# A decode kernel of attention and an MLP on one core: 16 of 128 partitions of two weight loads move from SyncE's DMA queue to GpSimd's

## The chip, the cores and the metric

The kernel runs on one core of a Trainium2 chip. The metric is the device time of one execution in microseconds (us). Three runs of the kernel before gave 213.38, 213.41 and 213.50 us; their median is 213.41 us.

## The reference, cut to what matters

There are four rows (a batch of 4, one token each) of width D = 576. After a layer norm, the result is the sum of the row, an attention part and an MLP part:

```python
xn = _layernorm(x)
return x + _A_ref(xn, A_k_cache, A_v_cache, A_wq, A_wo) + _B_ref(xn, B_w1, B_w2, B_w3, B_w4)

# attention: 32 query heads, 16 kv heads of width 128, a window of the last 2048 keys
p = softmax((xn @ wq) @ k.T * Dh ** -0.5);  o = p @ v;  return o @ wo
# MLP: the sequence has length 1, so that the shifted part hs is zero
x1 = x + hs
return x1 + _gelu(_layernorm(x1) @ w3) @ w4        # w3: 576 x 4608, w4: 4608 x 576
```

Nothing is shared between rows but the weights, and every byte of keys, values and weights is used once. All tensors are bf16.

## The kernel before, in words

**What is loaded.** All loads but that of x are issued by SyncE (SP in the profile), in one queue, in the order in which the program needs them. Large tiles (`wq`, `k`, `w3a`, `w3b`, `v`, `w4_end`) come from one pool, `big`, with four buffers of 4 MiB (NBUF = 4), so that a load is issued when the buffer that it takes has been given up by its last reader. The order of the pool is wq, k0, w3a, k1, w3b, k2 to k7, then eight pairs of value heads, then `w4_end`. `w3b` takes the buffer of `wq`, and k5 takes the buffer of `w3b`.

**The stages.** First q = xn @ wq (line 236). Then eight key tiles (line 512 on): each is transposed on VectorE in four pieces (line 297) and multiplied with q on TensorE (line 304). The MLP is put between the first key tiles. With tile 0, `w3a` is multiplied (first two of the four rows per partition, and the tail of w3; line 465 by way of `g_piece`); with tile 1, `w3b` (the second two rows), and then come gelu (line 467) and the first 12 of 36 rows per partition of w4, by `mlp_out` (line 395), which adds to an accumulator in PSUM. After the keys come softmax (line 309), the 16 value heads (line 384), `wo` in four pieces, and the other 24 rows of w4 in five pieces, of which the last four arrive at the very end (line 504 by way of `quad_out`). The sum is cast (line 579) and stored (line 580).

**The lines that the change touches.** For n == 1, line 521 takes a buffer for `w3b`, line 522 loads w3's second two rows per partition (`load_rows`, line 136: 128 partitions of 18,432 bytes, 2304 KB), and line 523 loads the first 12 rows of w4 behind them in the same buffer (`load_w4`, line 482: 128 partitions of 13,824 bytes, 1728 KB). Their readers are `g_piece` (line 526, over w3) and `mlp_out` (line 529, over w4[0]). GpSimd (POOL) issues no DMA before the change; it has eight short instructions, the last at 8.3 us.

**What sets the order.** In the part around the change the tile framework places the waits. A transfer waits for the last reader of the buffer it overwrites, and a matmul waits for the transfers that write what it reads. Within an engine, instructions run in program order. From line 539 on, TensorE's order is written out by hand.

Of the kernel before, what the change touches and what calls it, by code (L numbers as in the profile page):

```python
# [20 lines left out]
def kernel(  # L21
# [19 lines left out]
    nc = tc.nc  # L41
    P = 128
    B, Sq, D = A_x.shape
# [4 lines left out]
    F = B_w3.shape[1]  # L48
# [56 lines left out]
    def k_load(bp, kq, last=False):  # L105

        t = big.tile([P, CK, Dh], BF16, tag="big", name=f"k{bp}{kq}")
        lo = Sk - W + kq * 4 * CK
        src = k_rows[MT * bp:MT * bp + MT, lo:lo + 4 * CK, :].rearrange("m (q c) d -> m q (c d)", q=4)
        cuts = 2 if last else 1  # L110
        for a in range(cuts):
            n = CK * Dh // cuts
            nc.sync.dma_start(out=t[:].rearrange("p c d -> p (c d)")[:, a * n:(a + 1) * n], in_=src[:, :, a * n:(a + 1) * n])
        return t
# [12 lines left out]
    w3_src = B_w3[0:KJ * P, :].rearrange("(p j) f -> p j f", j=KJ)  # L127
    w4_src = B_w4.rearrange("(e m i) n -> e m i n", e=2, i=NFH)
# [3 lines left out]
    JR = 2  # L132

    def load_rows(t, a, src, j, n):

        nc.sync.dma_start(out=t[:, a:a + JR * n].rearrange("p (j n) -> p j n", j=JR), in_=src[:, j:j + JR, :])
        return [t[:, a + i * n:a + (i + 1) * n] for i in range(JR)]

    def load_tail(t, a, w, n):
        nc.sync.dma_start(out=t[:, a:a + n // 2], in_=w[KJ * P:D, :].rearrange("r (e f) -> (r e) f", e=2))  # L140
        return t[:, a:a + n // 2]
# [142 lines left out]
    def k_scores(n):  # L284

        bp, kq = K_order[n]
        kn = K_tiles.pop(n)
        if n == 0:
            S.extend(ps_s.tile([P, 512], F32, tag="S", name=f"S{g}") for g in range(4))
        C2 = CK // 2  # L290

        kt = [ktp.tile([P, C2, G, 2, 2], BF16, tag="kt", name=f"kt{n}{e}") for e in range(2)]
        last = n == len(K_order) - 1
        for i in range(4):
            a, e = divmod(i, 2) if last else (i % 2, i // 2)
            c0 = a * C2 // 2
            nc.vector.transpose(out=ap32(kt[e], c0 * 2 * G, [[2 * G, C2 // 2], [1, 2], [2, G]]),  # L297
                                in_=ap32(kn, c0 * 4 * G + e * G, [[4 * G, C2 // 2], [2 * G, 2], [1, G]]))
        for e in range(2):
            for t in range(2):  # L300
                y = 2 * e + t
                for m in range(NM):
                    c = 32 * (m % 4)
                    nc.tensor.matmul(out=S[kq][c:c + 32, :].rearrange("p (c q l) -> p c q l", q=4, l=2),  # L304
                                     lhsT=qz[:, bp, m, y, :], rhs=kt[e][:, :, 4 * m:4 * m + 4, :, t],
                                     start=(bp == 0 and m < 4 and y == 0), stop=(bp == 1 and m >= 4 and y == NY - 1),
                                     skip_group_check=True)
# [150 lines left out]
    def g_piece(t, j):  # L458
        for fc in range(NF):
            e, i = divmod(fc, NFH)  # L460
            if j < KJ:
                lhsT, rhs = t[:, e * (F // 2) + i:(e + 1) * (F // 2):NFH], ln2T[:, j, :]
            else:
                lhsT, rhs = t[:, i:F // 2:NFH], ln2T[:, KJ + e, :]
            nc.tensor.matmul(out=gp[:, fc, :], lhsT=lhsT, rhs=rhs, start=False, stop=False, skip_group_check=True)  # L465

    def gelu():
        xs = const.tile([P, NF, B], F32, name="g_x")
        nc.vector.tensor_copy(out=xs[:], in_=gp)
        u = const.tile([P, NF, B], F32, name="g_u")  # L470
        nc.vector.tensor_tensor(out=u[:], in0=xs[:], in1=xs[:], op=ALU.mult)
        nc.vector.tensor_scalar(out=u[:], in0=u[:], scalar1=GA, scalar2=1.0, op0=ALU.mult, op1=ALU.add)
        nc.vector.tensor_tensor(out=u[:], in0=u[:], in1=xs[:], op=ALU.mult)
        nc.scalar.activation(out=u[:], in_=u[:], func=ACT.Tanh, scale=GC)
        nc.vector.tensor_scalar(out=u[:], in0=u[:], scalar1=0.5, scalar2=0.5, op0=ALU.mult, op1=ALU.add)
        nc.vector.tensor_tensor(out=gT[:], in0=u[:], in1=xs[:], op=ALU.mult)
        nc.vector.tensor_copy(out=gTq[:, :, 0:G:NB], in_=gT[:, NFH:NFH + NQR, :])

    def load_w4(t, j0, e, i0, cuts):
        parts = []  # L480
        for m in cuts:
            nc.sync.dma_start(out=t[:, j0:j0 + m, :], in_=w4_src[e, :, i0:i0 + m, :])
            parts.append((t[:, j0:j0 + m, :], e, i0, m))
            j0 += m
            i0 += m
        return parts
# [20 lines left out]
    def mlp_out(t, e, i0, n, one=False):  # L507
        for i in range(n):
            acc_matmuls(gT[:, e * NFH + i0 + i, :], lambda a, z, i=i: t[:, i, a:z], 0 if one else i % 2)


    for n in range(len(K_order)):
        if n > 0:
            K_tiles[n] = k_load(*K_order[n], last=(n == len(K_order) - 1))
        w3 = []
        if n == 0:
            w3_a = big.tile([P, BIG], BF16, tag="big", name="w3a")
            w3 = list(enumerate(load_rows(w3_a, 0, w3_src, 0, F)))
            w3.append((KJ, load_tail(w3_a, JR * F, B_w3, F)))
        elif n == 1:  # L520
            w3_b = big.tile([P, BIG], BF16, tag="big", name="w3b")
            w3 = list(enumerate(load_rows(w3_b, 0, w3_src, JR, F), JR))
            w4 = load_w4(w3_b[:, JR * F:JR * F + 12 * D].rearrange("p (i n) -> p i n", n=D), 0, 0, 0, (12,))
        k_scores(n)
        for j, t in w3:
            g_piece(t, j)
        if n == 1:
            gelu()
            mlp_out(*w4[0], one=True)
# [81 lines left out]
```

## Time and profile before

| what | value |
|---|---|
| median of three runs | 213.41 us |
| span of the profiled execution, first to last instruction | 212.0 us |
| bytes moved, mean rate over the span | 87.32 MB, 412 GB/s |
| share of 16 DMA engines' span taken by SP's queue (q1) | 96.8% |
| busiest compute engine | DVE, 128.2 us (60%) |
| POOL | 1.8 us, 8 instructions |

The profiled execution has no time of its own beside its span; 213.41 - 212.0 = 1.4 us is what lies around the span (the launch ahead of the first instruction, and the end). A page of the profile gives each engine's busy time, a row of digits over 40 equal slices of the span, the DMA queues, the chain of work that ended last, and groups of instructions by line. "DMA share" is the mean busy share of the core's 16 DMA engines. The trace also holds a record of every DMA packet: its queue, size, start and duration, but not the engine that it ran on.

### The profile page before, as it was taken

The page shows a single profiled execution, that of the slowest core. Times are in us where ns is not written, and L with a number is a line of the kernel's source. Part 1 is how long each engine was busy: PE and PEld are TensorE (multiplying, and loading weights), DVE is VectorE, ACT ScalarE, POOL GpSimd, SP SyncE. Part 2 cuts the span into 40 slices and gives each one's busy share as a digit, 9 for nine tenths or more (in the row PEclk, how much of TensorE's full clock was granted, in tenths as well). Part 3 has the DMA queues.
Part 4 walks back from the last instruction along what each step waited for, and adds up shares of the span by engine and source line. Part 5 has one row for each costly group of instructions (what it writes and reads, how often), then busy time and mean ns, then how long its engine had stood idle before and what let it go on. Part 6 is the DMA issues. An engine that isn't in the chain of part 4 may idle for free. (4 is left out here: it accounts for less than half of the span.)

```text
span 212.0 us, 2539 instructions
## 1 busy us (share of the span) xinstructions
PE 98.4 (46%) x1071; PEld 50.5 (24%) x1071; DVE 128.2 (60%) x225; ACT 17.4 (8%) x35; POOL 1.8 (1%) x8
## 2 busy tenths in 40 slices
PE   1442059429903333423333421968573644555573
PEld 0111027408301011101111101734231321212241
DVE  7812592095349898979699916968475322145240
ACT  0004100000000000000000058730000000000000
POOL 2100000000000000000000000000000000000000
PEclk9999999999999999999999999999787555555555
DMA  7999999999999999999999999999999999999980
GB/s 261 427 457 433 411 442 454 392 420 460 420 420 457 411 445 433 408 451 399 433 427 420 436 415 432 436 423 423 426 430 417 434 415 438 423 427 419 423 356 18
DMA packets 5943, 87.32 MB, mean 412 GB/s; under 512 B 681, under 2 KB 685, under 8 KB 1453
## 3 DMA queue, kind: packets, MB, share of 16 engines
q1 hardware_dynamic: 5924, 87.17, 96.8%
q8 instruction: 8, 0.13, 0.3%
q14 instruction: 3, 0.02, 0.0%
q10 hardware_dynamic: 8, 0.00, 0.0%
HBM read 87.17 MB, written 0.00 MB: 411 GB/s over the span
## 5 line engine op out<-in xcount | busy, mean ns | idle before, releaser
L297 DVE STREAM_TRANSPOSE kt<-k 128x2048 int32<-128x2048 int32 x32 | 71.0, 2278 | 17.5 <-DMA k<-in_A_k_cache_dram 17.5
L304 PE MATMUL S<-kt,qz 128*32 128x512 bf16 x256 | 30.4, 622 | 56.9 <-DVE kt L297 56.9
L384 PE MATMUL O<-v,PZ 128*32 128x512 bf16 x256 | 23.6, 506 | 15.1 <-DMA v<-in_A_v_cache_dram 15.1
L304 PEld LDWEIGHTS <-qz 128*32 128x32 bf16 x256 | 9.5, 127 | 74.0 <-issue 67.5
L413 DVE TENSOR_SCALAR osum<-O,diag 128x128 f32<-128x128 f32 x16 | 5.6, 348 | 28.8 <-PE O L384 28.8
L415 DVE SCALAR_TENSOR_TENSOR osum<-O,diag,osum 128x128 f32<-128x128 f32 x48 | 16.5, 345 | 0.9
L384 PEld LDWEIGHTS <-PZ 128*32 128x32 bf16 x256 | 7.5, 116 | 22.5 <-DMA v<-in_A_v_cache_dram 12.6
L346 PE MATMUL pt<-ident,prs 128*128 128x128 bf16 x64 | 6.5, 287 | 10.1 <-DVE prs L342 10.1
L321 ACT ACTIVATE E<-S,nb 128x256 f32<-128x256 f32 x8 | 4.5, 704 | 69.9 <-DVE nb L318 69.9
L425 PEld LDWEIGHTS OT<-sel,osum 128*128 128x128 f32 x32 | 6.6, 258 | 13.5 <-issue 7.1
L425 PE MATMUL OT<-sel,osum 128*128 128x8 f32 x32 | 8.1, 326 | 3.4 <-DVE osum L415 3.4
L395 PE MATMUL ACC<-wo,onx 128*4 128x288 bf16 x64 | 4.5, 434 | 8.7 <-DVE onx L444 8.7
L346 PEld LDWEIGHTS <-prs 128*128 128x128 bf16 x64 | 5.8, 131 | 11.5 <-ACT prs L340 9.4
L342 DVE TENSOR_SCALAR prs<-E,rdm 128x512 bf16<-128x512 f32 x12 | 7.8, 801 | 0.0
L465 PEld LDWEIGHTS <-w3a 128*128 128x128 bf16 x108 | 6.9, 161 | 1.7 <-issue 1.7
L465 PE MATMUL ACC<-ln2T,w3a 128*128 128x4 bf16 x108 | 7.0, 202 | 0.0
L316 DVE TENSOR_REDUCE mx<-S 128x1 f32<-128x512 f32 x4 | 2.7, 681 | 5.4 <-PE S L304 5.4
L236 PE MATMUL qp<-wq,xnT 128*8 128x512 bf16 x32 | 3.8, 621 | 4.5 <-DMA wq<-in_A_wq_dram 4.5
L567 ACT COPY sums<-ACC 64x288 f32<-64x288 f32 x1 | 0.4, 393 | 64.5 <-PE ACC L395 64.5
L251 DVE CAST q_rows<-qp 128x256 bf16<-128x256 f32 x4 | 1.5, 420 | 5.9 <-PE qp L236 3.9
L340 ACT ACTIVATE prs<-E,rdm 128x512 bf16<-128x512 f32 x4 | 4.9, 1404 | 0.8 <-DVE rdm L328 0.8
L465 PEld LDWEIGHTS <-w3b 128*128 128x128 bf16 x72 | 4.5, 160 | 0.8 <-issue 0.8
(91 smaller groups left out, 68.1 us busy)
## 6 DMA issues: line engine op xcount, KB each, us to landing
v<-in_A_v_cache_dram SPq DMA_DIRECT2D x16, 2048.0 KB, 26.4
k<-in_A_k_cache_dram SPq DMA_DIRECT2D x7, 4096.0 KB, 30.6
wo<-in_A_wo_dram SPq DMA_DIRECT2D x4, 1152.0 KB, 29.8
wq<-in_A_wq_dram SPq DMA_DIRECT2D x2, 2048.0 KB, 12.9
k<-in_A_k_cache_dram SPq DMA_DIRECT2D x2, 2048.0 KB, 25.0
w3a<-in_B_w_dram SPq DMA_DIRECT2D x1, 2304.0 KB, 27.0
w3b<-in_B_w_dram SPq DMA_DIRECT2D x1, 2304.0 KB
w3b<-in_B_w_dram SPq DMA_DIRECT2D x1, 1728.0 KB, 34.6
```

The source lines that it names most:

```text
L297: nc.vector.transpose(out=ap32(kt[e], c0 * 2 * G, [[2 * G, C2 // 2], [1, 2], [2, G]]), in_=ap32(kn, c0 * 4 * G + e * G, [[4 * G, C2 // 2], ...
L304: nc.tensor.matmul(out=S[kq][c:c + 32, :].rearrange("p (c q l) -> p c q l", q=4, l=2), lhsT=qz[:, bp, m, y, :], rhs=kt[e][:, :, 4 * m:4 * ...
L321: nc.scalar.activation(out=E[:, :, g, x:GK:2].rearrange("p (c l) q -> p c q l", l=2), in_=S[g][:, 256 * x:256 * (x + 1)].rearrange("p (c q ...
L340: nc.scalar.mul(out=dst, in_=src, mul=rdm[:, b:b + 1])
L342: nc.vector.tensor_scalar_mul(out=dst, in0=src, scalar1=rdm[:, b:b + 1])
L346: nc.tensor.transpose(out=tp[:, cc, :], in_=pr[:, half * HC + cc, :, :, :].rearrange("p g k b -> p (g k b)"), identity=ident[:])
L384: nc.tensor.matmul(out=bank[G * j:G * j + G, :], lhsT=PZ[:, hp, c0:c0 + NI, :].rearrange("p c m -> p (c m)"), rhs=vn[:, c0:c0 + NI, :].rea ...
L395: nc.tensor.matmul(out=ACCS[half][o0:o0 + B, 0:DH], lhsT=lhsT, rhs=rhs_cols(q * DH, (q + 1) * DH), start=False, stop=False, skip_group_che ...
L413: nc.vector.tensor_scalar_mul(out=osum[:], in0=bank[:, 0:Dh], scalar1=diag[:, 0:1])
L415: nc.vector.scalar_tensor_tensor(out=osum[:], in0=bank[:, i * Dh:(i + 1) * Dh], scalar=diag[:, i:i + 1], in1=osum[:], op0=ALU.mult, op1=AL ...
L425: nc.tensor.matmul(out=OT[:, NB * o:NB * o + NB], lhsT=osum[:], rhs=sel[:], start=True, stop=True, skip_group_check=True)
L465: nc.tensor.matmul(out=gp[:, fc, :], lhsT=lhsT, rhs=rhs, start=False, stop=False, skip_group_check=True)
```

## The change

```diff
@@ -519,8 +519,16 @@
             w3.append((KJ, load_tail(w3_a, JR * F, B_w3, F)))
         elif n == 1:
             w3_b = big.tile([P, BIG], BF16, tag="big", name="w3b")
-            w3 = list(enumerate(load_rows(w3_b, 0, w3_src, JR, F), JR))
-            w4 = load_w4(w3_b[:, JR * F:JR * F + 12 * D].rearrange("p (i n) -> p i n", n=D), 0, 0, 0, (12,))
+            PM = P - 16
+            n2, n4 = JR * F, 12 * D
+            nc.sync.dma_start(out=w3_b[0:PM, 0:n2].rearrange("p (j n) -> p j n", j=JR), in_=w3_src[0:PM, JR:2 * JR, :])
+            nc.sync.dma_start(out=w3_b[0:PM, n2:n2 + n4].rearrange("p (i n) -> p i n", n=D), in_=w4_src[0, 0:PM, 0:12, :])
+            for p in range(PM, P):
+                nc.gpsimd.dma_start(out=w3_b[p:p + 1, 0:n2].rearrange("p (j n) -> p j n", j=JR), in_=w3_src[p:p + 1, JR:2 * JR, :])
+            for p in range(PM, P, 4):
+                nc.gpsimd.dma_start(out=w3_b[p:p + 4, n2:n2 + n4].rearrange("p (i n) -> p i n", n=D), in_=w4_src[0, p:p + 4, 0:12, :])
+            w3 = [(JR + i, w3_b[:, i * F:(i + 1) * F]) for i in range(JR)]
+            w4 = [(w3_b[:, n2:n2 + n4].rearrange("p (i n) -> p i n", n=D), 0, 0, 12)]
         k_scores(n)
         for j, t in w3:
             g_piece(t, j)
```

SyncE's two loads keep partitions 0 to 111. Partitions 112 to 127 come in GpSimd's queue: sixteen transfers of one partition (18,432 bytes each, w3), then four of four partitions (4 x 13,824 bytes each, w4). What is read, and where it is put, is the same.

## The prediction

> **What bounds the kernel now.** I read the page's slices first: is any engine busy all along?
>
> ```profile
> DVE  7812592095349898979699916968475322145240
> PEclk9999999999999999999999999999787555555555
> DMA  7999999999999999999999999999999999999980
> q1 hardware_dynamic: 5924, 87.17, 96.8%
> ```
>
> No compute engine is; the 16 DMA engines are, in 38 of 40 slices. The same by stages (columns: busy time of PE, weight loads, DVE, ACT, POOL, then granted clock, DMA share and GB/s):
>
> ```profile
> 16.50:33.00 16.50, 4.74 (x68) 3.40 (x69) 11.02 (x12) 3.40 (x9) 0.00 (x0) 1.00 1.01 433
> 33.00:48.00 15.00, 8.05 (x107) 5.67 (x106) 6.32 (x4) 0.00 (x0) 0.00 (x0) 1.00 0.98 418
> 110.00:142.00 32.00, 14.48 (x150) 8.69 (x145) 23.67 (x31) 13.23 (x24) 0.00 (x0) 1.00 1.00 425
> 170.00:205.00 35.00, 18.40 (x170) 8.40 (x173) 12.44 (x47) 0.00 (x0) 0.00 (x0) 0.50 1.00 422
> ```
>
> The share is 0.98 to 1.01 in each: the load stream never dries, and so the end is where the last DMA engine has moved its last byte. The end of the chain of work agrees:
>
> ```profile
> 154.84 32.51 DMA v<-in_A_v_cache_dram
> 187.34 0.02 issue
> 187.36 20.99 DMA w_end<-in_B_w_dram
> 208.35 0.04 issue
> 208.39 0.45 PE ACC L504 x8
> ```
>
> Last, the stream's end in steps of 1 us:
>
> ```profile
> 204.50:205.50 1.00, 1.00 (x32) 0.70 (x28) 0.13 (x1) 0.04 (x1) 0.00 (x0) 0.50 0.94 369
> 205.50:206.50 1.00, 1.00 (x36) 0.91 (x29) 0.32 (x1) 0.35 (x1) 0.00 (x0) 0.50 0.59 221
> 206.50:207.50 1.00, 0.88 (x28) 0.60 (x20) 0.00 (x0) 0.00 (x0) 0.00 (x0) 0.50 0.33 127
> 207.50:208.50 1.00, 0.66 (x20) 0.44 (x19) 0.00 (x0) 0.00 (x0) 0.00 (x0) 0.50 0.02 9
> ```
>
> The engines do not end together: the share falls to 0.59, 0.33 and 0.02, and by the packet records the last data packet ends at 207.9. From 204.5 on, 0.94 + 0.59 + 0.33 + 0.02 = 1.9 us of work per engine is left; shared evenly it would end at 206.4, 1.5 us earlier. So a microsecond more on the **last** engine costs one, and one on an early engine costs nothing.
>
> **The change, part by part.** The sum is made on the span, 212.0 us, and carried to the median by the 1.4 us around it, which I leave as they are.
>
> *Bytes.* None more or fewer: 16 x 18,432 + 16 x 13,824 = 516 KB change queues. In the packet records a load of 128 partitions is 128 data packets, one per partition: 688 ns for 18,432 bytes, 525 ns for 13,824. If SP's two loads still run on all engines alike, each engine has 7 rows instead of 8 and is relieved of 0.688 + 0.525 = 1.21 us; if POOL's rows go one to an engine, it gets the 1.21 us back. Sum 0.
>
> *Small packets.* SP's queue has 660 packets of 4 bytes (9 ns each) for 42 transfers: 16 for each of 41, and 4 for the store. The 4-partition load of x (ACT's queue) has 4 data packets and 4 such packets. So a transfer leaves one per engine that it runs on. SP's two transfers stay two. POOL's twenty add, by the row of x, 16 + 4 x 4 = 32 packets over 16 engines, 2 x 9 ns = 0.02 us on each; if each of the twenty runs on all engines, 20 x 9 = 0.18 us. In that case a row of 18,432 bytes also falls into 16 packets of 1152 bytes. Sizes 9216 (351 ns) and 18,432 (688 ns) give 14 ns per packet besides the bytes, so that sixteen such pieces cost an engine 16 x 14 - 14 = 0.21 us more than one whole row. Bounds 0.02 and 0.39; I take 0.2, the middle, since the row of x is near in kind but is of another queue.
>
> [...] No run here shows a GpSimd transfer.
>
> *Two queues on one engine.* The trace has one row of this kind: eight 16 KB packets of the instruction queue (q8) run between SP's. Beside each, the SP packet took longer: eight pairs, 467 to 660 ns more, mean 543, where 16,384 bytes alone take 616. So sharing costs between 0.15 us less and 0.05 us more than the bytes. An engine gets two large rows from POOL, so -0.3 to +0.1; if the price falls on each of twenty transfers, 20 x 0.05 = +0.9. I take 0, inside the nearest row's.
>
> *SP.* Two issues stay (0.33 and 0.43 us at 16.5). Nothing is added to its queue.
>
> *POOL.* Twenty issues from 16.5 us on, when `wq`'s buffer is free. POOL ends its last instruction at 8.8 and nobody waits for it later, so only `w3b`'s readers do. POOL's issue price is not in the trace. SP's issues run 0.33 to 0.65 us, so 20 take 7 to 13 us: done at 30. PE reads `w3b` at 48.33, so up to (48.3 - 16.5) / 20 = 1.6 us each costs nothing. Above it, see the second rival. Cost 0.
>
> *Order.* POOL's 516 KB overtake k0, w3a and k1, which SP has queued ahead: at 433 GB/s they land up to 1.2 us later. DVE waits 8.68 us for k1 and then 5.63 for k2, which hides it: k2 lands after the same sum of bytes as before. Without that cover it would cost 1.2. PE now waits for up to 22 transfers at `w3b` rather than two; some extra wait instructions of about 0.02 us each, on an engine that is idle half the time.
>
> *Sum:* 0 + 0.2 + 0 + 0 = +0.2 us: span 212.2, time **213.6 us**, with 213.1 (-0.3) to 214.7 (0.39 + 0.9) as this case's own bounds. This case has a chance of 0.45. A measurement of this kernel can tell about 0.2% (0.43 us) from no change, so this is mostly "within".
>
> **Rivals.**
>
> *Uneven engines: slower (0.25).* The sum of 0 for the bytes needs 16 equal shares, and no row shows how 112 partitions, or single ones, are dealt out. The place is the DMA engine that ends last; the price is one row, 0.688 or 0.525 us, for each row above its former eight; and it decides from the first such row on a late engine. If SP's loads leave some engines their 8 rows (and skip the last partitions' engines), the others get POOL's row on top: +1.2 + 0.2, **214.8 us**. If all POOL's rows fall on one engine: 16 x 0.688 + 4 x 4 x 0.525 = 19.4, less the 1.2 it is relieved of, **231 us**; with w4's four-row transfers on four engines, 16 x 0.688 + 4 x 0.525 - 1.2 = +11.9, 225. For it: nothing in the profile fixes the dealing. Against it: every 128-partition load here runs at a DMA share of 1.00, thus evenly, and x's four partitions made four equal shares. [...]
>
> *POOL is slow: slower (0.08).* Twenty serial issues ahead of `w3b`'s readers. Once `w3b` comes after about 59 us, DVE's second half of k2 (from 65.7) finds no buffer, since PE's scores of k1 stand behind `w3b`'s matmuls (4.6 + 1.9 us). DVE then has only 0.8 to 0.9 us of spare time per key tile and carries the delay to softmax. The stream first misses it when the value loads are issued at 142.3: by bytes issued (64.5 MB) against moved (428 GB/s from 1.8 us on: 60.1), 10 us of work is then left. So it decides at 69 us, 2.5 us an issue with 2 us for landing; at 3 us an issue the end is 9.5 us later, **223 us**. Against it: SP's 0.33 to 0.65.
>
> [...]
>
> *The last engine is relieved: faster (0.22).* The same dealing can go the other way: the engine that ends at 207.9 loses rows or an interruption, and POOL's go to those done at 205.4. The q8 packet at 205.6 took 1.1 us in the last microseconds; if PE's extra waits shift that fetch to another engine or moment, the end is some 0.5 to 0.8 us earlier. All skew gone gives -1.5. Time **212.6 us** (-0.8), from 212.1 to 213.0. For it: the skew is there, 0.59 and 0.33 at the end. Against it: nothing aims POOL's rows at early engines.
>
> That the two queues add bandwidth is excluded as a large gain: the share is 1.00 already and POOL's packets need the same 16 engines.
>
> **How the numbers follow.** Even shares 0.45 (within 0.30, slower 0.13, faster 0.02); uneven 0.25 (slower); slow POOL 0.08 (slower 0.06, within 0.02); relief 0.22 (faster 0.20, within 0.02). Faster 0.22, within 0.34, slower 0.44. The range runs from the relief case at 212.3 to the mild uneven case, 215.2; outside lie full relief and the heavy uneven and slow-POOL cases, about 0.18 together. The likeliest case's own range is 213.1 to 214.7.
>
> **What would show it.** Even shares: the packet records have 112 rows in SP's queue and 16 in POOL's, the share stays 1.00, and the last microseconds fall as before. Uneven: the tail of share below 0.6 grows longer than 3 us. Slow POOL: PE idles at line 465 for a DMA into `w3b`. Relief: the tail is shorter, with the last data packet before 207.3. What would make me wrong outright is a share under 0.97 in the stage from 16.5 to 48 us, where POOL's packets run: two queues that disturb each other.

## The result and the profile after

The changed kernel takes 236.8 us (median of 4 runs, 235.76 to 237.74) against 213.45 us (4 runs): a ratio of 1.109, 95% interval 1.105 to 1.112. It is slower by 23.3 us, far outside the predicted range. The span of its profiled execution is 235.3 us.

The slices of the page of the changed kernel (each 5.9 us) show two places that were not there before:

```profile
DMA  7999999999999999999999999932999999999990
GB/s 268 434 457 406 353 288 399 305 227 184 225 403 418 425 440 434 434 434 421 404 432 432 421 430 429 428 131 100 429 429 421 429 430 432 421 429 429 414 400 19
q1 hardware_dynamic: 5892, 86.65, 92.7%
q0 software_dynamic: 640, 0.52, 1.1%
```

From the fifth slice to the eleventh the rate falls to 184 to 399 GB/s, although the DMA digit stays at 9. In slices 27 and 28 the digit itself falls to 3 and 2. In the first of these places, called the slow stretch below, the engines are busy and the rate is low; in the second, the dry stretch, they have little to do. By stages (busy time of PE, weight loads, DVE, ACT, POOL, then granted clock as a share of full speed, DMA share, GB/s), for the changed kernel:

```profile
16.50:22.00 5.50, 0.67 (x16) 0.57 (x16) 1.71 (x6) 2.99 (x7) 3.85 (x8) 1.00 1.01 426
22.00:48.00 26.00, 10.69 (x140) 8.00 (x141) 9.12 (x5) 0.42 (x2) 5.90 (x12) 1.00 1.01 336
48.00:66.00 18.00, 3.80 (x32) 1.27 (x32) 8.89 (x4) 0.00 (x0) 0.00 (x0) 1.00 1.02 218
66.00:153.00 87.00, 30.89 (x296) 15.04 (x295) 63.94 (x49) 11.60 (x23) 0.00 (x0) 1.00 1.00 427
153.00:165.00 12.00, 9.27 (x102) 5.07 (x102) 7.31 (x21) 2.08 (x3) 0.00 (x0) 0.72 0.32 124
165.00:228.00 63.00, 33.18 (x360) 16.00 (x356) 25.99 (x100) 0.00 (x0) 0.00 (x0) 0.63 1.00 425
```

and for the kernel before, in the two stages that differ first:

```profile
22.00:48.00 26.00, 12.12 (x156) 8.50 (x156) 15.40 (x9) 0.62 (x3) 0.00 (x0) 1.00 0.99 420
48.00:66.00 18.00, 10.05 (x120) 6.71 (x120) 9.64 (x12) 0.32 (x1) 0.00 (x0) 1.00 1.01 435
```

The sum of what was lost, at 427 GB/s: (420 - 336) x 26 / 427 = 5.1 us from 22 to 48, (435 - 218) x 18 / 427 = 9.1 us from 48 to 66, and 12 x (1 - 124 / 427) = 8.5 us in the dry stretch; 22.7 of 23.3 us. Everywhere else the stream runs as before.

**The slow stretch.** The DMA share reads 1.01 and 1.02 there, so the engines do not idle; their packets are longer. In the packet records, SP's 112 packets of 13,824 bytes take 1144 ns on average, where they took 525. POOL's sixteen one-partition transfers are 256 packets of 1152 bytes, 16 from each, as many as there are engines (the records do not name the engine); its four-partition transfers are 16 packets of 13,824 bytes, 1131 ns each on average.

**The dry stretch.** Here TensorE did things in another order. The rows of tile w3b, in the kernel before:

```profile
L465 PE MATMUL ACC<-ln2T,w3b x72: 200/202/223, 48.3 to 52.8; 128*128 128x4 bf16 x72
L395 PE MATMUL ACC<-w3b,gT x24: 401/445/448, 55.3 to 57.9; 128*4 128x288 bf16 x24
```

and in the changed kernel:

```profile
L465 PE MATMUL ACC<-ln2T,w3b x72: 200/201/222, 139.0 to 143.4; 128*128 128x4 bf16 x72
L395 PE MATMUL ACC<-w3b,gT x24: 284/286/286, 166.3 to 167.7; 128*4 128x288 bf16 x24
```

The program's text has these matmuls behind key tile 1. The built program of the changed kernel has them behind key tile 7 and, for the last (line 395), behind the second pair of value heads: ahead of line 539 the tile framework orders TensorE itself, and it moved them. (Built, not run: with two GpSimd transfers instead of twenty the framework keeps the old order.) `w3b`'s buffer, one of four, was held to 167.7 us instead of 57.9. The DMA queue's own waits from 130 to 180 us of the changed kernel show what that does:

```profile
SPq L122 <- PE O L384: 25.0, 2, 23.6
```

SyncE waits 23.6 us in one piece to load values, until the first pair of value heads has been used (line 384) and its buffer is free. With one of the four buffers held, the other three did not bridge softmax: the DMA share is 0.32 from 153 to 165 us.

### The profile page after: what moved, and what is told of

Same layout as the page of the kernel before. It is cut to its first block, busy times and chain, and to the rows that moved or that the text cites. A ratio compares the mean times of both kernels' runs of the same rounds, so it can differ in the third digit from the quotient of the medians.

```text
span 235.3 us, 2575 instructions
## 1 busy us (share of the span) xinstructions
PE 98.2 (42%) x1071; PEld 50.3 (21%) x1071; DVE 127.6 (54%) x225; ACT 17.5 (7%) x35; POOL 11.8 (5%) x28
## 5 line engine op out<-in xcount | busy, mean ns | idle before, releaser
L384 PE MATMUL O<-v,PZ 128*32 128x512 bf16 x256 | 25.1, 529 | 17.4 <-DMA v<-in_A_v_cache_dram 17.4
L527 POOL DMA_DIRECT2D w3b<-in_B_w_dram x16 | 7.9, 500 | 18.8 <-DMA w3b<-in_B_w_dram 11.5
L342 DVE TENSOR_SCALAR prs<-E,rdm 128x512 bf16<-128x512 f32 x12 | 8.3, 788 | 0.0
```

What stands on the lines that cost most here:

```text
L342: nc.vector.tensor_scalar_mul(out=dst, in0=src, scalar1=rdm[:, b:b + 1])
L384: nc.tensor.matmul(out=bank[G * j:G * j + G, :], lhsT=PZ[:, hp, c0:c0 + NI, :].rearrange("p c m -> p (c m)"), rhs=vn[:, c0:c0 + NI, :].rea ...
L527: nc.gpsimd.dma_start(out=w3_b[p:p + 1, 0:n2].rearrange("p (j n) -> p j n", j=JR), in_=w3_src[p:p + 1, JR:2 * JR, :])
```

## The experiments

The two causes were stated as theories: slow packets (A) and the changed order (B). All fix TensorE's order by the same edit, so that only the loads differ; b1 alone has another order in it:

```diff
-    for n in range(len(K_order)):
+    with tc.manual_schedule(engines={mybir.EngineType.PE}):
+      for n in range(len(K_order)):
```

**Control, c0:** the loads of before, with this edit alone.

> The kernel before, with TensorE's order in the key loop written out by hand (scores of tile n, then the MLP's matmuls of tile n), as control for the next ones. Both theories: the loads are untouched and stay saturated, so 213.4 us, within 0.5.

Measured: 213.51 us, ratio 0.999 (0.998 to 1.001). The edit is free.

**Slow packets alone, a1:** the loads of the change, with this edit. (The expectations of a1 place the dry stretch at 138 to 148 us; that was misread from the slices, it is at 153 to 165.)

> The changed loads, with TensorE's order as in c0, so that w3b's buffer is given up after key tile 1 and not after the last one. Theory of two causes (slow packets while the new transfers run, and a dry stream at 138 to 148 us since w3b's buffer is held): the first stays, about +15.5 us (key tile 2 is transposed at 76.6 us instead of 61.2), the second goes; 229 us. Rival, that slow packets alone cause all of it and the dry stretch is their echo: 236 us as before.

Measured: 230.15 us, ratio 1.077 (1.074 to 1.081). The stages of a1:

```profile
16.50:66.00 49.50, 19.66 (x260) 14.35 (x260) 19.67 (x15) 3.41 (x9) 9.66 (x20) 1.00 1.01 297
66.00:220.00 154.00, 65.93 (x662) 31.20 (x662) 97.18 (x167) 13.51 (x25) 0.00 (x0) 0.67 1.00 426
```

The dry stretch is gone, the slow one is whole: with 429 GB/s as the mean of before's stages from 16.5 to 61, 49.5 x (1 - 297 / 429) = 15.2 us of the 16.6. The order is therefore worth 236.8 - 230.15 = 6.7 us of the 23.3. The sum by stages above has it otherwise, 14.2 us for the slow stretch and 8.5 for the dry one; the 2 us between the two ways of splitting are not explained.

**The order alone, b1:** the loads of before, with the later places for the MLP.

```diff
         k_scores(n)
-        for j, t in w3:
+        if n == 1:
+            w3_late = w3
+            continue
+        for j, t in w3:
             g_piece(t, j)
-        if n == 1:
-            gelu()
-            mlp_out(*w4[0], one=True)
+    for j, t in w3_late:
+        g_piece(t, j)
...
     PZ = softmax()
+    gelu()
...
             v_compute(v)
+            if v == 2:
+                mlp_out(*w4[0], one=True)
```

> The loads of before, all in SyncE's queue, with w3b's matmuls moved behind the last key tile and mlp_out behind the second value head, where the changed kernel has them on TensorE. Two causes: no slow packets, but a dry stretch near 120 to 135 us; 213.4 plus about 8 = 221 us. Rival (the order does not matter, only slow packets do): 213.4 us.

Measured: 217.9 us, ratio 1.020 (1.017 to 1.023). In b1 the stream is dry as well, though shorter than forecast:

```profile
136.00:143.00 7.00, 5.29 (x66) 3.66 (x66) 5.06 (x12) 2.75 (x3) 0.00 (x0) 1.00 0.55 234
```

So this order costs 4.4 us by itself, where about 8 were expected near 120 to 135 us, and the changed kernel's costs 6.7 on top of the slow packets. A and B are both shown, each without the other. b1 is not the changed kernel's order to the last instruction: its last MLP matmuls stand one value head earlier, and gelu's work on VectorE lies ahead of softmax's scaling (127.9 to 130.1 us), where the changed kernel has it in the midst of it (149.1 to 154.2). From the end of the last scores to the first value matmul are 17.2 us in b1 and 19.7 in the changed kernel. These 2.5 us are about what lies between 4.4 and 6.7, but no run tests that.

**Which transfers are slow.** First, s1: no GpSimd at all, SP's loads of 112 partitions and one SP transfer of 16 partitions each for the rest.

```diff
-            for p in range(PM, P):
-                nc.gpsimd.dma_start(out=w3_b[p:p + 1, 0:n2]...
-            for p in range(PM, P, 4):
-                nc.gpsimd.dma_start(out=w3_b[p:p + 4, n2:n2 + n4]...
+            nc.sync.dma_start(out=w3_b[PM:P, 0:n2]..., in_=w3_src[PM:P, JR:2 * JR, :])
+            nc.sync.dma_start(out=w3_b[PM:P, n2:n2 + n4]..., in_=w4_src[0, PM:P, 0:12, :])
```

> SyncE's loads of 112 partitions as in the change, the other 16 partitions in SyncE's queue too, as one transfer of 16 partitions each; nothing in GpSimd's queue; order as in c0. If 112 partitions dealt 7 to an engine disturb each other: the 13,824-byte packets still take about 1100 ns instead of 525, and 6 to 10 us are lost, 220 to 223 us. If GpSimd's queue is what disturbs: packets at 525 and 688 ns, 213.5 us.

Measured: 224.54 us, ratio 1.051 (1.046 to 1.056), a little above the expected 220 to 223. Two thirds of A's 16.6 us come without GpSimd. Packets of w4 take 1031 ns on average, up to 2320; those of w3b up to 2940.

s4 is the same with the 16-partition transfers issued by GpSimd (`nc.gpsimd` for `nc.sync` in the last two lines).

> SyncE's loads of 112 partitions as in the change; the other 16 partitions in GpSimd's queue as one transfer of 16 for w3 and one for w4, order as in c0. If the number of partitions in a transfer matters and not the queue: as with SyncE issuing them, 224.5 us. If GpSimd's queue or its many small transfers cost by themselves, 230 us as with the change's twenty.

Measured: 225.79 us, ratio 1.058 (1.054 to 1.061): 1.2 us more than with SP, 4.4 less than with twenty transfers. Here the queue matters little, the shape more.

h64 has SP load each of the two as partitions 0 to 63 and 64 to 127: 4 rows for each of 16 engines, if they are dealt evenly.

> All in SyncE's queue: each of the two loads as two transfers of 64 partitions (0 to 63, 64 to 127); order as in c0. Theory of shared write paths: 16 engines then write only half of the paths, every packet of w3b and w4 takes about twice as long (1370 and 1050 ns), 8 x (0.69 + 0.53) = 9.7 us lost, 223 us. Rival, that 7 rows an engine or 112 as a count is what is slow: 4 rows an engine are even, 213.6 us.

Measured: 223.84 us, ratio 1.049 (1.041 to 1.057). The packets of w3b take 1378 ns where 688 is usual, those of w4 1041 where 525 is: doubled, within 2%. The stages of h64, ahead of these loads, in them, and behind:

```profile
22.00:39.00 17.00, 8.18 (x104) 5.69 (x105) 9.12 (x5) 0.33 (x2) 0.00 (x0) 1.00 1.00 425
40.00:60.00 20.00, 9.81 (x127) 7.11 (x126) 9.25 (x6) 0.00 (x0) 0.00 (x0) 1.00 1.03 218
66.00:100.00 34.00, 9.78 (x84) 3.00 (x80) 25.50 (x12) 0.00 (x0) 0.00 (x0) 1.00 1.00 430
```

Half the partitions, half the rate (218 against 425 and 430 GB/s), at a DMA share of 1.03 and with SP as the only issuer: in this run the rate went by the partitions a transfer takes. Why it halves is not shown. In all these runs the rows read from memory go with the partitions written, so the runs do not tell a limit of writing from one of reading, and the expectation's shared write paths stay a theory.

x112 adds one SP transfer of 112 partitions, 2.06 MB, into `wo`'s buffers (made one tile here, idle until about 100 us) behind whole loads; its data is not used.

```diff
             w4 = load_w4(w3_b[:, JR * F:JR * F + 12 * D]...
+            spare = WO[:].rearrange("p a n -> p (a n)")
+            nc.sync.dma_start(out=spare[0:112, :], in_=w3_src[0:112, JR:2 * JR, :].rearrange("p j n -> p (j n)"))
```

> SyncE's loads of w3b and w4 whole, and one more in SyncE's queue behind them, of 112 partitions of w3's rows into a buffer that nobody reads (wo's): 2.06 MB more, at the usual 688 ns a packet 7 x 0.69 = 4.8 us. Order as in c0. Theory (112 partitions dealt 7 to an engine make engines meet on write paths, without any other transfer): its packets take 1050 to 1150 ns, 213.5 + 7 x 1.1 = 221 us. Rival, that only the transfers of 16 partitions or fewer disturb: 688 ns, 218.3 us.

Measured: 222.75 us, ratio 1.042 (1.040 to 1.045), above the theory's 221 too. Its 112 packets take 1152 ns on average: 256 others of that size at 688, all 368 at 829. So this load of 112 partitions is slow with nothing small beside it. Of the 9.1 us, 4.8 are bytes. The expectation's theory, that at seven rows each engines meet on write paths, fits this, but the records do not name the engine, so it is not shown.

**GpSimd's small transfers alone.** In s2, s3 and s3x, SP's loads are whole, and GpSimd's go into the same idle buffer from the same time on; their data is not used. (No run has the one `wo` tile without an added load; behind 66 us these runs and x112 move 424 to 430 GB/s, about as the kernel before does.)

```diff
+            nc.gpsimd.tensor_copy(out=spare[:, 0:4], in_=q_rows[:, 0, 0, 0, 0:4])
+            for p in range(P - 16, P):                          # s2
+                nc.gpsimd.dma_start(out=spare[p:p + 1, :]..., in_=w3_src[p:p + 1, JR:2 * JR, :])
+            for p in range(P - 16, P, 4):                       # s3
+                nc.gpsimd.dma_start(out=spare[p:p + 4, 0:12 * D]..., in_=w4_src[0, p:p + 4, 0:12, :])
+            for p in range(P - 16, P - 12):                     # s3x
+                nc.gpsimd.dma_start(out=spare[p:P:4, 0:12 * D]..., in_=w4_src[0, p:P:4, 0:12, :])
```

> SyncE's loads of w3b and w4 whole, 128 partitions, as before; beside them GpSimd's sixteen one-partition transfers of the change, from the same time on, into a buffer that nobody reads (wo's, idle until 100 us). 295 KB more are moved, 0.7 us. Order as in c0. Theory that engines which write the same few partitions block each other: each such transfer is dealt to all 16 engines and all write one partition, 16 x 0.69 = 11 us of one write path, with everything behind it; SyncE's packets beside them are longer, 5 us lost before key tile 1 is there, about 219.5 us. Rival, that only loads of 112 partitions are slow: 214.2 us.

s2 measured: 220.04 us, ratio 1.031 (1.028 to 1.034); 6.5 us, of which 0.7 are bytes. Right in size.

> As the run before, with GpSimd's four four-partition transfers of w4 instead of the sixteen (221 KB more, 0.5 us). Same theory: four engines each write four neighbouring partitions and take about 1.1 us a packet instead of 0.53, 1 to 2 us lost on some engines, 215 to 216 us. Rival: 214.0 us.

s3 measured: 221.96 us, ratio 1.040 (1.037 to 1.043). 8.5 us, against 1 to 2 expected: the direction held and the size did not. The expectation priced GpSimd's own packets; the cost lies in SP's. In the records the four packets of such a transfer start within 41 ns of one another and take 0.62 to 0.87 us each. Beside the first, sixteen of SP's packets of 32,768 bytes take 2.6 to 3.1 us where 1.21 is usual; beside the second, sixteen of 18,432 bytes take 1.8 to 2.3 us where 0.69 is, and beside the third and fourth up to 2.4 and 2.6. Over all SP packets of these two sizes that is 6.5 us an engine of the 8.5 lost.

> As the run with four four-partition transfers beside whole loads (221.96 us), the same bytes and the same number of transfers, but each transfer takes every fourth partition (112, 116, 120, 124; then 113, ...) instead of four neighbours. Theory that neighbouring partitions in groups of four share a write path: the four rows of a transfer no longer meet, the paths are held about a quarter as long, 8.4 us of loss shrinks to about 2, 215.5 us. Rival, a price per small GpSimd transfer or per engine that gets one: 222 us as before.

s3x measured: 217.6 us, ratio 1.018 (1.016 to 1.020), between the theory's 215.5 and the rival's 222. The same bytes, issuer and number of transfers as in s3; only the partitions of one transfer are no neighbours, and more than half of the cost goes (3.9 us left of 8.5). SP's packets of the two sizes lose 1.9 us an engine instead of 6.5. That neighbouring partitions matter in these two runs is shown; that they are all of the cost is not. From 20 to 35 us, s3 first:

```profile
20.00:35.00 15.00, 2.57 (x32) 1.30 (x33) 9.35 (x8) 1.09 (x5) 0.00 (x0) 1.00 0.98 227
```

and s3x:

```profile
20.00:35.00 15.00, 3.65 (x44) 1.78 (x48) 9.78 (x8) 1.30 (x6) 0.00 (x0) 1.00 1.00 369
```

**The same offload, cut by columns, p128:** GpSimd loads the last 4 of w4's 12 rows for all 128 partitions in one transfer.

```diff
-            w4 = load_w4(w3_b[:, JR * F:JR * F + 12 * D]..., 0, 0, 0, (12,))
+            nc.sync.dma_start(out=t4[:, 0:8, :], in_=w4_src[0, :, 0:8, :])
+            nc.gpsimd.dma_start(out=t4[:, 8:12, :], in_=w4_src[0, :, 8:12, :])
```

> About the same bytes in GpSimd's queue as in the change (590 KB), cut by columns: the last 4 of the 12 rows of w4 for all 128 partitions in one transfer, w3 and the first 8 rows in SyncE's queue for all 128; order as in c0. Theory of shared write paths: each engine writes its own paths in either queue, packets at their usual length (4608 bytes about 180 ns), nothing lost, 213.5 us within 0.6. Rival, that a second queue beside SyncE's costs by itself: 215 us or more.

Measured: 213.62 us, ratio 1.000 (0.999 to 1.001). GpSimd's 128 packets of 4608 bytes take 179 ns, as SP's do (178 in the kernel before). Its stages:

```profile
16.50:33.00 16.50, 2.57 (x32) 1.30 (x33) 10.47 (x11) 3.41 (x9) 0.46 (x1) 1.00 1.02 435
33.00:48.00 15.00, 8.75 (x128) 7.43 (x131) 4.92 (x4) 0.00 (x0) 0.00 (x0) 1.00 0.97 412
```

A second queue as such, with one transfer in it, cost nothing and brought nothing here (213.62 us against 213.69 for the kernel before). No version tried beats the kernel before.

## Why the prediction was wrong, point by point

**What bounds the kernel** was right: the load stream, with no slack (a DMA share of 0.98 to 1.01 by stages in the kernel before). That is why each lost microsecond showed: 22.7 us lost in the stream, 23.3 in the time.

**"Bytes ... Sum 0"** is the step that failed first. It took a packet's 688 and 525 ns as the price of a row wherever and in whatever company it is written. All rows that I had, but for the four small ones of x, were of 128-partition loads, and I carried them over to 112, 4 and 1 partitions. SP's packets measured 1144 ns (w4, 525 before), and A costs 16.6 us instead of 0. The upper end of 214.7 us (0.39 + 0.9) bounded nothing here, because its rows did not come from large transfers that cover part of the partitions.

**"Two queues on one engine"** was priced by instruction fetches; p128 shows that the price was indeed nil for one transfer of all 128 partitions (ratio 1.000). It was not the question. One reading was off: seven of the eight fetches show a longer SP packet beside them, by 467 to 548 ns, on average 504; the 660 stands beside an 8 KB packet of another queue (q14).

**"Small packets"**: the sixteen did fall into 16 pieces each, and GpSimd's queue has 368 packets of 4 bytes. At 9 to 13 ns and 23 to an engine that is at most 0.3 us, and 16 pieces of 66 ns are 0.37 us more than one whole row, where 0.21 was priced: the right order, and of no weight.

**"Order"** failed second. I counted up to 22 waits of TensorE at `w3b` instead of two and took its order as given, although the trace of before had shown matmuls of w3a between two halves of one key tile: an order that the program text does not have, so a scheduler's:

```profile
28.93 1.90 PE L304 MATMUL S<-kt,qz 128*32 128x512 bf16 x16 [7.70 <-DVE kt L297]
30.76 4.63 PE L465 MATMUL ACC<-ln2T,w3a 128*128 128x4 bf16 x72
35.32 1.90 PE L304 MATMUL S<-kt,qz 128*32 128x512 bf16 x16
```

The front part says that instructions run in program order there; for TensorE ahead of line 539 they run in the order that the framework chose. This step cost 6.7 us; b1's order, near to it, cost 4.4 alone.

**"POOL"** had the price of an issue right, 0.49 to 0.68 us, but not the end: the last was done at 41.8 instead of 30, because after eight issues it began to wait for landings (11.5 us in six waits at line 527):

```profile
16.31 4.04 POOL L527 DMA_DIRECT2D w3b<-in_B_w_dram  x8 [7.33 <-PE qp L236]
23.84 0.49 POOL L527 DMA_DIRECT2D w3b<-in_B_w_dram  x1 [3.50 <-DMA w3b<-in_B_w_dram]
```

That is still ahead of 48.3, where TensorE read `w3b` before.

**The rivals.** "Uneven engines" had the right term, that nothing in the profile fixes how small transfers are dealt out, and the wrong price. It priced how many rows an engine gets; what counted in h64 (packets of 1378 ns for 688), in x112 (1152 for 688) and in s3 against s3x (8.5 against 3.9 us) is which partitions a transfer takes. "POOL is slow" named the right consequence, a value load that comes too late behind softmax, for the wrong reason. The tail stayed much as it was: shares of 0.99, 0.57 and 0.12 in the last microseconds, 0.94, 0.59 and 0.33 before. **"What would make me wrong outright"** was a share under 0.97 from 16.5 to 48 us. It read 1.01 there, with the rate at 352 GB/s where it was 426: the share stayed while packets grew longer (SP's of 18,432 bytes in that window from 688 to 938 ns on average). The rate was the column to name.

What stays open: the trace does not say which engine moved a packet, so shared write paths stay the author's theory, which the times of h64, s3 against s3x and p128 fit, and reading is not told apart from writing. The parts do not add up: s1's 11.0 and the 5.8 and 7.9 us of s2 and s3 beyond their bytes make more than A's 16.6. Why four packets a transfer in s3 hold up sixteen of SP's was not settled, nor why s3x keeps 3.9 us, 0.5 of them bytes.

## What to carry to other kernels

Cut a load by columns and keep all 128 partitions: on a saturated stream 590 KB moved to another queue that way cost nothing, and 516 KB cut by partitions cost 16.6 us. Carry a packet's duration over to no other shape of transfer: 13,824 bytes took 525 ns in a load of 128 partitions, 1041 in one of 64. Judge a DMA stage by GB/s: from 48 to 66 us the busy share read 1.02 at 218 GB/s in the changed kernel and 1.01 at 435 in the kernel before. And where a framework orders an engine, compare the built order before and after an edit to a load: twenty small transfers moved TensorE's work by six key tiles, and the buffer it held cost 6.7 us.

## What was not expected of the hardware

Four transfers of four neighbouring partitions, 221 KB in all, cost the whole stream 8.5 us (s3): their own packets take 0.9 us at most, while SP's beside them take up to 1.9 us longer each. Loads of 64 partitions ran at half the rate of loads of 128 (218 against 425 to 430 GB/s, h64).
